# A Fourier mix and gated feed-forward kernel on one Trainium2 core: its first load units moved to partitions 16 to 111, and four edits beside it

## The chip, the cores and the metric

The kernel runs on one NeuronCore of a Trainium2 chip. The metric is the device time of one execution in microseconds (us), the median of several runs. The kernel before takes 2854.43 us (median of 3 runs, 2854.14 to 2856.18).

## What is computed

Two steps, all in float32. First a Fourier mix over the sequence of 3008 tokens, for 8 batches of 256 channels; then a feed-forward layer on the 24064 tokens that come out.

```python
X = np.fft.rfft(x, axis=1)                    # x: (8, 3008, 256)
Yr = Xr @ w_r - Xi @ w_i + b_r                # w_r, w_i: (256, 256)
Yi = Xr @ w_i + Xi @ w_r + b_i
Yr = np.sign(Yr) * np.maximum(np.abs(Yr) - 0.01, 0.0)
Yi = np.sign(Yi) * np.maximum(np.abs(Yi) - 0.01, 0.0)
y = np.fft.irfft(Yr + 1j * Yi, n=3008, axis=1)
gate = 1.0 / (1.0 + np.exp(-(y @ w_gate)))    # w_gate, w_val: (256, 1536)
val = y @ w_val
out = gate * val @ w_out                      # w_out: (1536, 256)
```

## The kernel before

The transform of length 3008 is split as 47 x 64. **Product a** (`fwd_a`, `product_a`, the line that the profile names `pa`) multiplies a unit of x by the 47-point table `fa_sb` on TensorE. A unit is a tile `xf` of 94 partitions (47 points x 2 halves) by 4 x 256 values, some 4 KB for each partition; a batch has 8 units. A unit takes two matmuls of 512 columns, each written to one PSUM bank (tag `fft`, three banks in turn) and copied back over the unit, the first by ScalarE, the second by VectorE, as 96 partitions. `store_a` then writes the unit to a DRAM buffer `zd`. **Step b** (`load_b`, `fwd_b`, tiles `zf` and `pb`) reads `zd` across all eight units, so its first load must wait until all eight units of its batch have been stored. It is followed by the mix with w_r and w_i (`mix4`, tile `pm`), the soft threshold and the inverse step (`inv_b`, tile `pi`), whose results go to `vd`. The last inverse product (`inv_a`, tile `pia`) reads `vd` as tiles `vf`, and makes the columns of y. Batch 0 goes through b, mix and inverse in 14 steps q, with batch 1's first product done beside it.

The feed-forward weights arrive as raw 64-bit words, in 18 parts of 512 KB (`load_part`, tiles `raw`), and VectorE and ScalarE make float32r high and low parts of them in some ten operations each (`from_f64`: the ops "exp", "top", "low" and so on). Seven parts go through the buffers of batch 0's units during the 14 steps, the eighth through the pool `big` (five buffers, which batch 1's units use as well). The others are loaded in the first chunk of the feed-forward, one for each of its 12 sub-steps f. `converting`, called three times in each `ffn1`, finishes the part in hand and starts the next; it stands ahead of the sigmoid in ScalarE's queue.

Since PE waits in the first chunk for weights, the first product of batches 2 and 3 is mixed in as filler: 32 **half units** (`load_half`, `half_a`; tiles `xfh` of 94 x 512 and `azh`, a ring of three buffers with tag `st`, stored by GpSimd's queue). `AT_FIRST` of them run ahead of the chunk's first `inv_a`; the others follow in the sub-steps.

The order of this part is written out by hand (`tc.manual_schedule()`): each engine runs its instructions in program order, and so does SP, which issues nearly all loads and stores. An instruction that waits holds everything behind it on its engine or queue. Fourteen matmuls on zeros (`warm`, `WARM`) stand ahead of the first product.

The lines in question:

```python
def load_a(b, h):                                             # L165
    xf = p0.tile([P, 4, D], F32, name="xf0", bufs=R1 // 8) if b == 0 else big("xf")
    for lo_, hi_ in ((0, 64), (64, 2 * R2)):
        nc.sync.dma_start(xf[lo_:hi_], xv[b, lo_:hi_, 4 * h:4 * h + 4])
...
    for h in range(na):                                       # L833
        load_a(0, h)
    load_a(1, 0)
    for h in range(na):
        fwd_a(0, h)
        store_a(0, h)
        if h in (1, 3, 4):
            load_a(1, {1: 1, 3: 2, 4: 3}[h])
```

Of the kernel before, what the change touches and what calls it, by code (L numbers as in the profile page):

```python
# [9 lines left out]
F32 = mybir.dt.float32  # L10
# [9 lines left out]
R2, R1 = 47, 64  # L20
NK2 = 24
NQ = 2 * NK2
# [9 lines left out]

SIDE_GAP = 14
PRE = 2
WARM = 14
EARLY = 4
AT_FIRST = 4
NCONV = 7


# [23 lines left out]
def _tables(seq):  # L64
    n2 = np.arange(R2)
    k2 = np.arange(NK2)
    c, s = _cs(n2[:, None] * k2[None, :], R2)
    fa = np.zeros((R2, 2, NK2, 2, 2))
    fb = np.zeros((NK2, 2, 2, 128))
    for j in range(2):  # L70
        fa[:, j, :, 0, j] = c
        fa[:, j, :, 1, j] = -s
        fb[:, 0, j, j:2 * R2:2] = c.T / seq
        fb[:, 1, j, j:2 * R2:2] = -s.T / seq
    fa = fa.reshape(2 * R2, 2 * NQ)
    fb = fb.reshape(2 * NQ, 128).astype(np.float32)
    n1 = np.arange(R1)
    k1 = np.arange(R1)
    mf = np.zeros((NK2, 128, 128), np.float32)
    mi = np.zeros((NK2, 128, 128), np.float32)  # L80
    mis = np.zeros((NK2, 128, 2, 128), np.float32)
    for q in range(NK2):
        k = q + R2 * k1
        c, s = _cs(n1[:, None] * k[None, :], seq)
        flip = np.where(k > seq // 2, -1.0, 1.0)
        m = np.zeros((2, R1, 2, R1))
        m[0, :, 0] = c
        m[1, :, 0] = s
        m[0, :, 1] = -s * flip
        m[1, :, 1] = c * flip  # L90
        w = np.full(R1, 2.0)
        if q == 0:
            w[k > seq // 2] = 0.0
            w[(k == 0) | (2 * k == seq)] = 1.0
        e = np.zeros((2, R1, 2, R1))
        e[0, :, 0] = (w * c).T
        e[1, :, 0] = (-w * flip * s).T
        if q:
            e[0, :, 1] = (w * s).T
            e[1, :, 1] = (w * flip * c).T  # L100
        mf[q] = m.reshape(128, 128)
        mi[q] = e.reshape(128, 128)
        mis[q, :, 0], mis[q, :, 1] = _split(e.reshape(128, 128))
    return {"mf": mf, "mi": mi, "mis": mis, "fa": fa.astype(np.float32), "fb": fb}


@with_exitstack
def tile_fft_mix_ffn(ctx: ExitStack, tc, x, w_r, w_i, b_r, b_i, w_one, w_out, mf, mi, mis, fa, fb, out):
    nc = tc.nc
    B, S, D = x.shape  # L110
    P = 128
    CT = D // P
    NF = w_one.shape[0]
# [14 lines left out]
    p0 = p0s.enter_context(tc.tile_pool(name="p0", bufs=1, side="right"))  # L128
# [8 lines left out]
    def bank(name, tag="fft", bufs=FFT_BANKS):  # L137
        return (psf if tag == "fft" else psl).tile([P, 512], F32, tag=tag, bufs=bufs, name=name)
# [5 lines left out]
        return p2.tile([P, 2, D], F32R, tag="r2k", bufs=NR2K, name=name)  # L144

    fa_sb = cw.tile([2 * R2, 2 * NQ], F32, name="fa_sb")
    nc.scalar.dma_start(fa_sb, fa)

    zd = [tc.dram_tile([NQ, R1, D], F32, name=f"zd{b}") for b in range(B)]
    vd = [tc.dram_tile([NQ, R1, D], F32, name=f"vd{b}") for b in range(B)]  # L150
# [1 line left out]
    md = tc.dram_tile([NK2, P, 2, P], F32, name="md")  # L152
    yd = tc.dram_tile([CT, P, B * S - T0], F32, name="yd").rearrange("t p n -> p t n")
    xv = x.rearrange("b (n2 j h) c -> b (n2 j) h c", j=2, h=R1 // 2)
    zv = [z.rearrange("q (j h) c -> (q j) h c", j=2) for z in zd]
    vv = [v.rearrange("q (j h) c -> (q j) h c", j=2) for v in vd]

    held = {}
# [3 lines left out]
    def big(name):  # L162
        return p2.tile([P, 4, D], F32, tag="big", bufs=NBIG, name=name)

    def load_a(b, h):  # L165
        xf = p0.tile([P, 4, D], F32, name="xf0", bufs=R1 // 8) if b == 0 else big("xf")
        for lo_, hi_ in ((0, 64), (64, 2 * R2)):
            nc.sync.dma_start(xf[lo_:hi_], xv[b, lo_:hi_, 4 * h:4 * h + 4])
        held["x", b, h] = xf

    def product_a(xi, az, copy):
        pa = bank("pa")[:2 * NQ]
        nc.tensor.matmul(pa, fa_sb, xi, start=True, stop=True)  # L173
        copy(az, pa.rearrange("p (h c) -> p h c", h=2))

    def fwd_a(b, h):

        xf = held["x", b, h]
        for i in range(2):
            at = slice(2 * i, 2 * i + 2)  # L180
            product_a(xf[:2 * R2, at], xf[:2 * NQ, at], nc.vector.tensor_copy if b < 2 and i else nc.scalar.copy)

    def store_a(b, h, queue=nc.sync):
        queue.dma_start(zv[b][:, 4 * h:4 * h + 4], held.pop(("x", b, h))[:2 * NQ])

    def load_half(b, h):
        xf = r2k("xfh").bitcast(F32)
# [105 lines left out]
    def inv_b(b, q, m, full):  # L293
        pi = bank("pi")
        y = held.pop(("ys", b, q))
        for i in range(2):
            o = pi[:, i * D:(i + 1) * D]
            if full:
                nc.tensor.matmul(o, m[:, i], y[:, i], start=True, stop=True)
            else:  # L300
                yh, yl = y
                nc.tensor.matmul(o, m[:, i, 0], yh[:, i], start=True, stop=False)
                nc.tensor.matmul(o, m[:, i, 0], yl[:, i], start=False, stop=False)
                nc.tensor.matmul(o, m[:, i, 1], yh[:, i], start=False, stop=True)
        vz = p2.tile([P, 2, D], F32, tag="st", bufs=NST, name="vz")
        nc.scalar.copy(vz, pi.rearrange("p (q d) -> p q d", q=2))
        (nc.gpsimd if full else nc.sync).dma_start(vd[b][4 * q:4 * q + 4].rearrange("(q a) n d -> (a n) q d", q=2), vz)
# [514 lines left out]
    def halves(upto):  # L822

        while waiting:
            i = len(beside) - len(waiting)
            if i >= upto:
                break
            half_a(*waiting.pop(0))
            if i + NR2K < len(beside):
                load_half(*beside[i + NR2K])  # L830

    with tc.manual_schedule():
        for h in range(na):  # L833
            load_a(0, h)
        load_a(1, 0)
        for h in range(na):
            fwd_a(0, h)
            store_a(0, h)
            if h in (1, 3, 4):
                load_a(1, {1: 1, 3: 2, 4: 3}[h])  # L840
            if h == 2:
                load_mix()
        mfs[0] = load_mf(0)
        for q in range(2):
            load_b(0, q)
        load_bias4()
        mfs[1] = load_mf(1)
        for h in range(EARLY):
            fwd_a(1, h)
            if h == 1:  # L850
                wi_sb = mix_weights()
        for q in range(NP + 2):
            if q + 2 < NP:
                load_b(0, q + 2)
            if 0 <= q - 1 < NP:
                mis_[q - 1] = load_mi(q - 1, True)
            if q < 2:
                for h in range(q * EARLY // 2, (q + 1) * EARLY // 2):
                    store_a(1, h)
                load_part()  # L860
            if q == 3:
                nc.sync.dma_start(fb_sb, fb)
                load_bias()
            if len(parts) > 3 * NF // 2 - NCONV and q > 2 and q % 2 or q == NP:
                load_part()
            if q % 2 == 0 and 4 <= q < 4 + 2 * (na - EARLY):
                load_a(1, EARLY + q // 2 - 2)
            if q < NP:
                fwd_b(0, q, mfs[q], True)
            if q + 2 < NP:  # L870
                mfs[q + 2] = load_mf(q + 2)

            if q % 2:
                ops("sum word", 0)
                start_part(p0)
                ops("exp low top", -1)
            elif q:
                ops("power mant", -1)
                if len(started) > 1:
                    ops("hi lo", 0)  # L880
                ops("one", -1)
            if q == 4:
                sub(bias_sb[:, 1], bias_sb[:, 1], bias_sb[:, 0])
            if 0 <= q - 1 < NP:
                mix4(0, q - 1)
            if q == NP + 1:

                fwd_a(1, EARLY)
                store_a(1, EARLY, nc.gpsimd)
            if 0 <= q - 2 < NP:  # L890
                inv_b(0, q - 2, mis_[q - 2], True)

        for bh in beside[:NR2K]:
            load_half(*bh)
        left = ["hi lo", "power mant one", "sum word", "hi lo"]
        for h in range(EARLY + 1, na):
            ops(left.pop(0), 0)
            fwd_a(1, h)
            store_a(1, h, nc.gpsimd)
        ops(left.pop(0), 0)  # L900
    p0s.close()
    p3 = p3s.enter_context(tc.tile_pool(name="p3", bufs=2, side="right", reuse_waits="tile"))
    with tc.manual_schedule():
        for u in own0:
            load_v(u)
        halves(AT_FIRST)
        for f in range(NF):
            ffn[f]()
            if f in (2, 3):
                tables[f - 2, 1] = load_mi(f - 2, False)  # L910
            halves(AT_FIRST + (f + 1) * (len(beside) - AT_FIRST) // NF)
            if parts:
                load_part()
    hook.clear()


# [127 lines left out]
```

## Time and profile before

| | |
|---|---|
| median of 3 runs | 2854.43 us (2854.14 to 2856.18) |
| the profiled execution, own time | 2852.08 us |
| its span, first to last instruction | 2850.3 us |
| PE (TensorE matmul) busy | 2812.0 us, 99% |
| VectorE (DVE) busy | 2085.8 us, 73% |
| ScalarE (ACT) busy | 1318.3 us, 46% |
| GpSimd (POOL) busy | 709.1 us, 25% |
| mean granted TensorE clock | 0.996 of full speed |

The profile is one execution; times within it count from the span's start, and the execution's own time is 1.8 us more than the span. Everything that the change touches happens in the first 205 us. Busy shares hide waits there, so the views to read are the ones by stretch, the waits of PE, and the chain of work that ended last, which goes back from the last instruction to what released each step.

### The profile page before, as it was taken

The numbers are of one execution on the slowest core, as the hardware profiler recorded it, in microseconds if no ns is written. First come the engines' busy times: TensorE is split into PE (matmuls) and PEld (weight loads), VectorE is DVE, ScalarE is ACT, GpSimd is POOL, SyncE is SP. The second block draws the span as 40 slices with busy tenths as digits, with TensorE's granted clock in tenths as the row PEclk, the third lists the DMA queues.
The fourth block names the chain that finished last, engine by engine and source line by source line (L and its number), as shares of the span: only waits on it lengthen the run. The fifth ranks groups of instructions, "written<-read, shape, count | busy, mean of one in ns | idle before, by whom it ended". The sixth has DMA issues, their size and how long they took to land.

```text
span 2850.3 us, 38265 instructions
## 1 busy us (share of the span) xinstructions
PE 2812.0 (99%) x13882; PEld 2308.8 (81%) x13882; DVE 2085.8 (73%) x3110; ACT 1318.3 (46%) x2293; POOL 709.1 (25%) x638
## 2 busy tenths in 40 slices
PE   8899999999999999999999999999999999999999
PEld 6668888888899977888888888888888888888887
DVE  5668777667778625777777777777777777777776
ACT  4565555454455433444444444444444444444443
POOL 0211000003900001323333333333333333333321
PEclk9999999999999999999999999999999999999999
DMA  9776544655654471000000000000000000000000
GB/s 274 224 220 190 171 144 136 178 168 179 215 155 145 144 231 54 16 15 30 30 30 15 16 30 30 16 15 30 30 30 15 16 30 30 16 15 30 30 16 15
DMA packets 174509, 240.49 MB, mean 84 GB/s; under 512 B 15792, under 2 KB 126096, under 8 KB 174320
## 3 DMA queue, kind: packets, MB, share of 16 engines
q1 hardware_dynamic: 164816, 214.41, 24.5%
q0 software_dynamic: 9408, 23.60, 2.6%
q8 instruction: 110, 1.80, 0.3%
q14 instruction: 79, 0.65, 0.1%
q10 hardware_dynamic: 96, 0.04, 0.0%
HBM read 133.65 MB, written 104.33 MB: 83 GB/s over the span
## 4 chain that ended last, share of the span: by engine, by line
PE 91%; DVE 4%; DMA 3%; ACT 1%; issue 1%; SPq 0%; POOL 0%; ACTq 0%; DVEq 0%; POOLq 0%
PE pd L635 11%; PE pc L635 11%; PE pa L635 11%; PE po L607 7%; PE po L606 7%; PE po L605 7%; PE pb L635 5%; PE pm L265 5%; PE pia L334 3%; PE pb L231 3%; PE pa L173 3%; PE po L411 1%; PE po L412 1%; PE po L413 1%; PE pv L388 1%; PE pv L386 1%
## 5 line engine op out<-in xcount | busy, mean ns | idle before, releaser
L607 PE MATMUL po<-hl,w 128*128 128x512 f32 x912 | 362.5, 398 | 0.0
L606 PE MATMUL po<-hh,w 128*128 128x512 f32 x912 | 361.6, 397 | 0.0
L605 PE MATMUL po<-hh,w 128*128 128x512 f32 x912 | 360.8, 396 | 0.0
L694 POOL TENSOR_TENSOR c<-c,c 128x512 f32<-128x512 f32 x114 | 147.2, 1291 | 807.7 <-DVE c L690 633.8
L635 PE MATMUL pc<-s,w1h 128*128 128x512 f32 x912 | 284.1, 393 | 2.8 <-DVE v L669 2.8
L635 PE MATMUL pa<-a,w1h 128*128 128x512 f32 x912 | 284.2, 393 | 0.5 <-ACT u L661 0.5
L690 DVE TENSOR_TENSOR c<-u,pc 128x512 f32<-128x512 f32 x228 | 156.6, 687 | 115.5 <-PE pc L635 106.9
L665 DVE TENSOR_TENSOR u<-u,pb 128x512 f32<-128x512 f32 x228 | 155.3, 681 | 88.9 <-PE pb L635 62.7
L585 ACT CAST hh<-v 128x512 fp32r<-128x512 f32 x114 | 70.7, 620 | 306.2 <-DVE v L675 306.2
L607 PEld LDWEIGHTS po<-hl,w 128*128 128x128 f32 x912 | 171.5, 188 | 41.9
L605 PEld LDWEIGHTS po<-hh,w 128*128 128x128 f32 x912 | 172.0, 189 | 41.0
L635 PEld LDWEIGHTS pa<-a,w1h 128*128 128x128 f32 x912 | 171.1, 188 | 41.0 <-ACT u L661 0.9
L635 PEld LDWEIGHTS pc<-s,w1h 128*128 128x128 f32 x912 | 170.8, 188 | 41.3 <-DVE v L669 4.1
L606 PEld LDWEIGHTS po<-hh,w 128*128 128x128 f32 x912 | 171.0, 188 | 40.7
L589 POOL TENSOR_TENSOR hl<-c,hh 128x512 fp32r<-128x512 f32 x114 | 152.3, 1336 | 186.1 <-ACT hh L585 186.1
L265 PE MATMUL pm<-w_sb,xsh 128*128 128x256 f32 x1008 | 189.2, 287 | 0.3 <-DVE ys L271 0.3
L635 PE MATMUL pc<-s,w1l 128*128 128x512 f32 x456 | 177.4, 389 | 0.0
L635 PE MATMUL pa<-a,w1l 128*128 128x512 f32 x456 | 177.0, 388 | 0.0
L696 DVE TENSOR_TENSOR u<-u,pd 128x512 f32<-128x512 f32 x228 | 156.8, 688 | 24.5 <-DVE c L690 0.9
L667 DVE TENSOR_TENSOR v<-u,pd 128x512 f32<-128x512 f32 x228 | 156.8, 688 | 24.4 <-DVE u L665 0.5
L669 DVE TENSOR_TENSOR v<-v,pc 128x512 f32<-128x512 f32 x228 | 156.7, 687 | 24.4 <-DVE v L667 0.9
L661 ACT COPY u<-pa 128x512 f32<-128x512 f32 x228 | 133.7, 586 | 79.5 <-PE pa L635 79.3
(164 smaller groups left out, 6762.1 us busy)
## 6 DMA issues: line engine op xcount, KB each, us to landing
zf<-zd SPq DMA_DIRECT2D x96, 256.0 KB, 3.6
vf<-vd SPq DMA_DIRECT2D x128, 192.0 KB, 3.2
out_dram<-ot SPq DMA_DIRECT2D x94, 256.0 KB, 2.1
vd<-vz SPq DMA_DIRECT2D x84, 256.0 KB, 2.8
ypair<-yd SPq DMA_DIRECT2D x19, 1024.0 KB, 4.9
yd<-yf SPq DMA_DIRECT2D x103, 188.0 KB, 3.0
zd<-xf SPq DMA_DIRECT2D x44, 384.0 KB, 3.7
xf<-in_x_dram SPq DMA_DIRECT2D x48, 256.0 KB, 4.4
```

The costliest lines, as they stand in the source:

```text
L265: nc.tensor.matmul(o, l, r, start=(i == 0), stop=(i == len(mms) - 1))
L589: sub_(hl, h, hh)
L605: nc.tensor.matmul(o, wh, hh, start=(f == 0), stop=False)
L606: nc.tensor.matmul(o, wl, hh, start=False, stop=False)
L607: nc.tensor.matmul(o, wh, hl, start=False, stop=(f == NF - 1))
L635: nc.tensor.matmul(o, l, r, start=not more and l is wh and r is xh, stop=l is wl, skip_group_check=more)
L665: add(u, u, b)
L667: add(v, u, d)
L669: add(v, v, c)
L690: add(c12, u, c)
L694: nc.gpsimd.tensor_mul(c12, g12, c12)
L696: add(u, u, d)
```

## The change

- The units of batch 0, and the first four of batch 1, are loaded by one DMA of 96 rows to partitions 16 to 111, in place of two of 64 and 30 rows to partitions 0 to 93. Partitions 0 to 15 are set to zero by a memset (VectorE for the odd units of batch 0, GpSimd for all others), and the product uses a table `fa0_sb` of 128 x 128, shifted by 16 and with zeros around. The product now has 110 rows and 112 columns of weights, and its copies have 112 partitions. Of the 96 rows the last two belong to the next batch, and their table rows are not used. The other units still use `fa_sb`, which is now loaded in step q = 3.
- In SP's queue the first unit of batch 1 no longer stands ahead of the first store; batch 1's units follow stores 0, 2, 4 and 6, and w_r and w_i follow store 3.
- `WARM` goes from 14 to 10.
- One more weight part, the ninth, is loaded ahead of the chunk: after the 14 steps and before the first half units' loads. In the chunk the load of a part moves ahead of the half units of its sub-step.
- `AT_FIRST` goes from 4 to 3, so that 29 and not 28 half units run within the chunk.

```diff
-WARM = 14
+WARM = 10
 EARLY = 4
-AT_FIRST = 4
+AT_FIRST = 3
+AT0 = 16
...
+    fa0 = np.zeros((128, 128))
+    fa0[AT0:AT0 + 2 * R2, AT0:AT0 + 2 * NQ] = fa
...
     def load_a(b, h):
-        xf = p0.tile([P, 4, D], F32, name="xf0", bufs=R1 // 8) if b == 0 else big("xf")
+        xf = big("xf")
...
+    TOP = AT0 + 2 * NQ
+
+    def load_a0(b, h, clear):
+        xf = p0.tile([P, 4, D], F32, name="xf0", bufs=R1 // 8) if b == 0 else big("xf")
+        clear(xf[:AT0], 0.0)
+        at = b * 2 * R2
+        nc.sync.dma_start(xf[AT0:TOP], xr[at:at + 2 * NQ, 4 * h:4 * h + 4])
+        held["x", b, h] = xf
+
+    def fwd_a0(b, h):
+        xf = held["x", b, h]
+        for i in range(2):
+            at = slice(2 * i, 2 * i + 2)
+            product_a(xf[:AT0 + 2 * R2, at], xf[:TOP, at], nc.vector.tensor_copy if i else nc.scalar.copy,
+                      fa0_sb[:AT0 + 2 * R2, :TOP])
+
+    def store_a0(b, h):
+        nc.sync.dma_start(zv[b][:, 4 * h:4 * h + 4], held.pop(("x", b, h))[AT0:TOP])
...
         for h in range(na):
-            load_a(0, h)
-        load_a(1, 0)
+            load_a0(0, h, (nc.vector if h % 2 else nc.gpsimd).memset)
         for h in range(na):
-            fwd_a(0, h)
-            store_a(0, h)
-            if h in (1, 3, 4):
-                load_a(1, {1: 1, 3: 2, 4: 3}[h])
-            if h == 2:
+            fwd_a0(0, h)
+            store_a0(0, h)
+            if h % 2 == 0:
+                load_a0(1, h // 2, nc.gpsimd.memset)
+            if h == 3:
                 load_mix()
...
             if q == 3:
+                nc.sync.dma_start(fa_sb, fa)
                 nc.sync.dma_start(fb_sb, fb)
...
                 inv_b(0, q - 2, mis_[q - 2], True)
+        load_part()
 
         for bh in beside[:NR2K]:
             load_half(*bh)
...
-            halves(AT_FIRST + (f + 1) * (len(beside) - AT_FIRST) // NF)
             if parts:
                 load_part()
+            halves(AT_FIRST + (f + 1) * (len(beside) - AT_FIRST) // NF)
```

SP's queue at the start, from the last unit of batch 0 on, in the kernel before (`xf_145` is that unit, `xf` are units of batch 1, `xf_124` to `xf_130` the first three of batch 0, `zd_77` batch 0's buffer in DRAM; behind "waits" stand the semaphores of the queues and engines waited for):

```order
L168 DMA xf_145<-in_x_dram 64x1024 [waits DMAHW7_49]
L168 DMA xf_145<-in_x_dram 30x1024 [waits DMAHW0_49]
L168 DMA xf<-in_x_dram 64x1024 [waits DMAHW1_49]
L168 DMA xf<-in_x_dram 30x1024 [waits DMAHW2_49]
L184 DMA zd_77<-xf_124 96x1024 [waits DMAHW3_49,DVE_49,Activation_49]
L184 DMA zd_77<-xf_127 96x1024 [waits DMAHW4_49,DVE_49,Activation_49]
L168 DMA xf<-in_x_dram 64x1024 [waits DMAHW5_49]
```

The same place in the kernel changed (`xf_142` is the last unit, `xf_121` to `xf_130` the first four, `zd_78` the buffer):

```order
L200 DMA xf_142<-in_x_dram 96x1024 [waits DMAHW0_49]
L211 DMA zd_78<-xf_121 96x1024 [waits DMAHW1_49,DVE_49,Activation_49]
L200 DMA xf<-in_x_dram 96x1024 [waits DMAHW2_49]
L211 DMA zd_78<-xf_124 96x1024 [waits DMAHW3_49,DVE_49,Activation_49]
L211 DMA zd_78<-xf_127 96x1024 [waits DMAHW4_49,DVE_49,Activation_49]
```

Eight issues stand ahead of the first store now, where eighteen stood, and no load of batch 1 is among them.

SP's queue between the 14 steps and the first chunk, before (`raw` is a weight part, `xfh` a half unit, `vf` a load of `vd` for `inv_a`):

```order
L784 DMA raw<-in_w_out_dram 128x1024
L189 DMA xfh<-in_x_dram 64x512 [waits DMAHW2_49]
L189 DMA xfh<-in_x_dram 30x512 [waits DMAHW3_49]
...
L189 DMA xfh<-in_x_dram 30x512 [waits DMAHW1_49]
L317 DMA vf<-vd_85 96x512 [waits DMASW5_49,DMASW4_49,DMASW6_49,DMASW3_49,DMASW7_49,DMASW2_49,DMAHW2_49,DMASW1_49,DMASW0_49]
```

The same place now:

```order
L811 DMA raw<-in_w_out_dram 128x1024 [waits Pool_49]
L811 DMA raw<-in_w_one_dram 128x1024 [waits DMASW3_49,DMAHW7_49,DVE_49,Activation_49]
L216 DMA xfh<-in_x_dram 64x512 [waits DMAHW0_49]
L216 DMA xfh<-in_x_dram 30x512 [waits DMAHW1_49]
...
L216 DMA xfh<-in_x_dram 30x512 [waits DMAHW7_49]
L344 DMA vf<-vd_86 96x512 [waits DMASW5_49,DMASW6_49,DMASW4_49,DMASW7_49,DMASW2_49,DMAHW0_49,DMASW1_49,DMASW0_49]
```

The ninth part stands between the eighth and the half units' eight loads. It takes the `big` buffer of batch 1's fifth unit, and so waits for that unit's store on GpSimd's queue (DMASW3); the half units and the `vf` loads are queued behind it.

ScalarE's queue ahead of the chunk, before (`azh` are the copies of half units, `yth` the first operand of the feed-forward):

```order
L174 COPY azh<-pa 96x512 [waits DMASW1_49,PE_49]
L174 COPY azh<-pa 96x512 [waits DMASW2_49,PE_49]
L174 COPY azh<-pa 96x512 [waits DMASW4_49,PE_49,Activation_49]
L174 COPY azh<-pa 96x512 [waits DMASW0_49,PE_49]
L326 CAST yth<-pia 128x2x188 [waits PE_49] x2
```

And now:

```order
L181 COPY azh<-pa 96x512 [waits DMASW1_49,PE_49]
L181 COPY azh<-pa 96x512 [waits DMASW2_49,PE_49]
L181 COPY azh<-pa 96x512 [waits DMASW4_49,PE_49,Activation_49]
L353 CAST yth<-pia 128x2x188 [waits PE_49] x2
```

The fourth copy, which waited for the store of the first one's buffer (DMASW0), is no longer ahead of `yth`.

## Rows read from the trace of the kernel before

**Rows 1.** The page's part 5, a GpSimd operation: busy us, mean ns | idle, releaser.

```profile
L694 POOL TENSOR_TENSOR c<-c,c 128x512 f32<-128x512 f32 x114 | 147.2, 1291 | 807.7 <-DVE c L690 633.8
```

**Rows 2.** Stretches: length; busy us of each engine; PEclk, DMA share, GB/s.

```profile
2.20:14.00 11.80, 11.80 (x32) 6.04 (x31) 2.54 (x4) 3.61 (x5) 0.00 (x0) 1.00 1.00 247
33.38:43.00 9.62, 8.44 (x40) 8.18 (x41) 1.81 (x3) 4.13 (x8) 0.00 (x0) 0.54 0.93 304
43.00:95.80 52.80, 51.40 (x393) 48.79 (x392) 45.68 (x80) 34.47 (x63) 7.63 (x11) 1.00 0.85 255
130.10:134.57 4.47, 4.46 (x13) 3.50 (x14) 3.72 (x8) 2.82 (x6) 1.40 (x3) 0.62 0.39 126
205.00:2850.00 2645.00, 2627.34 (x13035) 2177.20 (x13034) 1960.96 (x2896) 1202.01 (x2083) 678.53 (x582) 1.00 0.23 72
```

**Rows 3.** Waits of PE, 0 to 210 us: releaser, total, times, longest.

```profile
PE pv L386 <- ACT sg L392: 4.0, 2, 3.7
PE pb L231 <- DMA zf<-zd: 3.7, 1, 3.7
PE pia L334 <- ACT azh L174: 3.0, 3, 2.0
...
PE pg L388 <- DVE w1l L770: 0.9, 1, 0.9
```

**Rows 4.** Timeline of PE, 0 to 13 us: start, length, instruction.

```profile
1.46 5.00 PE L811 MATMUL warm<-zero 128*128 128x512 f32 x14 [1.46 <-DVE ebias L817]
6.29 7.19 PE L173 MATMUL pa<-xf,fa_sb 94*96 94x512 f32 x16
```

**Rows 5.** Timeline of SP's queue, the issues of three stretches.

```profile
0.74 11.35 SPq L168 DMA_DIRECT2D xf<-in_x_dram  x18
12.66 0.79 SPq L184 DMA_DIRECT2D zd<-xf  x2
...
22.33 2.06 SPq L184 DMA_DIRECT2D zd<-xf  x3
...
93.06 4.58 SPq L189 DMA_DIRECT2D xfh<-in_x_dram  x8
...
103.28 1.44 SPq L317 DMA_DIRECT2D vf<-vd  x3
```

**Rows 6.** The DMA view, 22.5 to 29.5 us.

```profile
DMA packets 832, 2.56 MB, mean 366 GB/s; under 512 B 136, under 2 KB 217, under 8 KB 832
```

**Rows 7.** The chain that ended last, 20 to 45 us: start, length, what.

```profile
24.09 6.27 DMA zd<-xf
...
30.50 2.75 DMA zf<-zd
```

**Rows 8.** The chain, 104 to 131 us.

```profile
111.81 2.03 PE pia L334 x8
...
115.58 0.43 PE pg L388
...
117.62 0.23 PE pv L387
...
122.61 5.60 DMA raw<-in_w_one_dram
```

**Rows 9.** GpSimd's store of batch 1's fifth unit: its issue, and its time to landing.

```profile
98.94 0.55 POOL L184 DMA_DIRECT2D zd<-xf  x1 [2.59 <-ACT xf L174]
...
DMA to landing us min/median/max: 3.2/3.2/3.2
```

**Rows 10.** Time to landing: half unit loads issued at 93.1 and 93.6, then last two vf.

```profile
DMA to landing us min/median/max: 3.9/4.1/4.3
...
DMA to landing us min/median/max: 4.9/4.9/5.0
```

**Rows 11.** Timeline of PE, 102 to 115 us.

```profile
103.66 3.60 PE L173 MATMUL pa<-xfh,fa_sb 94*96 94x512 f32 x8
...
114.31 0.79 PE L386 MATMUL pg<-yth,w1h 128*128 128x512 f32 x1 [0.47 <-ACT yth L326]
```

More of the change, by code (lines that the diff above doesn't have):

```diff
@@ L76, in _tables @@
     fb = fb.reshape(2 * NQ, 128).astype(np.float32)
+    fa0 = np.zeros((128, 128))
+    fa0[AT0:AT0 + 2 * R2, AT0:AT0 + 2 * NQ] = fa
+    fa0 = fa0.astype(np.float32)
     n1 = np.arange(R1)
@@ L103, in _tables, with tile_fft_mix_ffn @@
         mis[q, :, 0], mis[q, :, 1] = _split(e.reshape(128, 128))
-    return {"mf": mf, "mi": mi, "mis": mis, "fa": fa.astype(np.float32), "fb": fb}
+    return {"mf": mf, "mi": mi, "mis": mis, "fa0": fa0, "fa": fa.astype(np.float32), "fb": fb}
 @with_exitstack
-def tile_fft_mix_ffn(ctx: ExitStack, tc, x, w_r, w_i, b_r, b_i, w_one, w_out, mf, mi, mis, fa, fb, out):
+def tile_fft_mix_ffn(ctx: ExitStack, tc, x, w_r, w_i, b_r, b_i, w_one, w_out, mf, mi, mis, fa0, fa, fb, out):
     nc = tc.nc
@@ L146, in tile_fft_mix_ffn @@
     fa_sb = cw.tile([2 * R2, 2 * NQ], F32, name="fa_sb")
-    nc.scalar.dma_start(fa_sb, fa)
+    fa0_sb = p0.tile([P, P], F32, name="fa0_sb")
+    nc.scalar.dma_start(fa0_sb, fa0)
     zd = [tc.dram_tile([NQ, R1, D], F32, name=f"zd{b}") for b in range(B)]
@@ L154, in tile_fft_mix_ffn @@
     xv = x.rearrange("b (n2 j h) c -> b (n2 j) h c", j=2, h=R1 // 2)
+    xr = x.rearrange("b (n h) c -> (b n) h c", h=R1 // 2)
     zv = [z.rearrange("q (j h) c -> (q j) h c", j=2) for z in zd]
@@ L169, in load_a, with product_a @@
         held["x", b, h] = xf
-    def product_a(xi, az, copy):
-        pa = bank("pa")[:2 * NQ]
-        nc.tensor.matmul(pa, fa_sb, xi, start=True, stop=True)
+    def product_a(xi, az, copy, table=None):
+        pa = bank("pa")[:az.shape[0]]
+        nc.tensor.matmul(pa, fa_sb if table is None else table, xi, start=True, stop=True)
         copy(az, pa.rearrange("p (h c) -> p h c", h=2))
@@ L848, in tile_fft_mix_ffn @@
         for h in range(EARLY):
-            fwd_a(1, h)
+            fwd_a0(1, h)
             if h == 1:
@@ L858, in tile_fft_mix_ffn @@
                 for h in range(q * EARLY // 2, (q + 1) * EARLY // 2):
-                    store_a(1, h)
+                    store_a0(1, h)
                 load_part()
             if q == 3:
+                nc.sync.dma_start(fa_sb, fa)
                 nc.sync.dma_start(fb_sb, fb)
```

## The prediction

> **What bounds it now.** I read the busy time by stretch first. From 205 us to the end PE is busy for 2627 of 2645 us at full clock [rows 2]: what is won or lost ahead of that moves the end by as much, and little can be won behind it. So the question is PE's losses in the first 205 us, and the waits of PE name three [rows 3]: 3.7 us for `zf`, the first load of step b; 3.0 us for ScalarE's copies of half units (2.0 of it at one place, ahead of the first chunk); and 3.7 us of one wait for a sigmoid in the chunk. Next I read the clock. From 33.38 to 43.0 us PE's mean clock is 0.54, that is nearly all at 1.2 GHz in place of 2.4, after the wait for `zf`; from 130.10 to 134.57 it is 0.62, after the wait for the sigmoid [rows 2]. The 14 steps of batch 0 between them (43.0 to 95.8 us) keep PE busy for 51.4 of 52.8 us. Last, the chain says what each wait hangs on.
>
> At the start it is the last store of batch 0, issued at 24.09 and landed 6.27 us later; then `zf`, issued at 30.50 and landed in 2.75 [rows 7]. The store is late because DMA is full: from 2.2 to 14 us, nearly all x loads, its share is 1.00 at 247 GB/s [rows 2], while from 22.5 to 29.5 us, mostly stores of 96 partitions, 366 GB/s flow [rows 6]. Besides, SP issues loads until 12.1 us and the first store at 12.66 [rows 5]. In the chunk the chain goes through a raw part, issued at 122.61, landing after 5.60 us [rows 8]: ScalarE stood waiting for it with the sigmoid behind.
>
> **The start.** Ahead of the last store's landing stand 12 unit loads of 385 KB, 8 stores of 393 KB and 0.52 MB of w_r and w_i, 8.3 MB. The new loads have 96 rows, so it becomes 12 x 0.393 + 8 x 0.393 + 0.52 + 0.07 (the table) = 8.46 MB. What rate do loads of 96 rows get? No row shows them alone. Bounds: 247 GB/s, as the loads of 64 and 30 rows get now, and 400, a tenth above the 366 of the stores [rows 2, 6]; I take 366, since the new loads have the stores' shape (96 partitions, 4 KB each). From 2.2 us on, 8.46 MB / 366 take 23.1 us, so 25.3. The 8.3 MB of now, 13.8 us at 247 and the other 4.9 MB at 366, end at 29.4, and the last store lands at 24.09 + 6.27 = 30.4 [rows 7], 1.0 us behind its data; so the store lands at 26.3. `zf` takes 0.14 + 2.75 + 0.13 us as now [rows 7], and step b starts at 29.3 in place of 33.38: **-4.1 us**. At 400 GB/s VectorE's six weight operations ahead of the last unit copies decide, at about 27.7: -5.7. With loads at 247 and the rest at 366, 19.1 + 10.2 us of data: +2.1.
>
> PE is no bound of this. Its warm-up takes 1.46 to 6.46 us for 14 matmuls [rows 4]; at 0.23 us for each of the last four, as at full clock [rows 8], 10 end near 5.5. From 6.29 on the product runs at 7.19 / 8 = 0.90 us [rows 4], two to a unit, so the last unit of batch 0 is done near 20, and its store lands only at 26.3. The shorter warm-up would save its 0.9 us at most, and I count nothing: DMA is the cover, and if that went, 0.9 us would be gained. The products follow the warm-up without a gap in either kernel, so the clock should rise as it does now.
>
> The memsets: GpSimd's two-input operation on 512 columns takes 1.29 us [rows 1], so one of 1024 columns takes at most 2.6; four end by 11 us, and the unit of the last is needed near 16. VectorE's first copy is due at 6. Copies of 112 partitions in place of 96, and 110 rows in the product, have the same columns: nothing. `fa_sb` at q = 3 is one more issue on SP, in a stretch with DMA share 0.85 [rows 2]: nothing, and 0.5 us if it lands on a needed `zf`.
>
> With the wait shorter (PE's products end near 27, `zf` comes at 29.3) the clock may fall later or not at all. But the second and third product of step b hang on loads behind it in SP's queue, so I count **-0.5 us** of the slow stretch, between 0 and -2.
>
> **Ahead of the chunk.** Here SP is made to wait. The ninth part waits for the fifth unit's store, issued at 98.94 and landed 3.2 us later [rows 9], so at 102.1. Behind it are the half units' eight issues, 4.58 us [rows 5], which ran at 93.06 and now start at 102.5. The first half unit lands about 4.3 us later [rows 10], near 106.8; PE has run out of work at 103.66 [rows 11] and stands for 3 us. The `vf` loads, issued at 103.28 now [rows 5], come at 107.1; the last of three takes 1.0 us to its issue and 4.9 to land [rows 10], 113.0. The third `pia`, which waits for the fourth half unit's copy and runs at 111.81 now [rows 8], starts there: what the removed copy gives, the `vf` load takes back, and the chunk starts **+1.2 us** late. It stays slow for longer after such a pause: before, seven of the first twelve matmuls take 0.43 us and five 0.23 [rows 8]; with all at 0.43, **+1.0**. The half unit moved into the chunk, where PE has no gap, costs two matmuls of 0.43 us, **+0.9**.
>
> In return the ninth part is there when the second sub-step asks for it, and the 3.7 us go [rows 3]: **-3.7**. The stretch at 1.2 GHz behind it, 4.47 us for twelve matmuls, becomes 12 x 0.23 = 2.8 [rows 2, 8]: **-1.7**. What is late next is PE itself: a sub-step has 18 matmuls of 0.23 us and two or three half units, and the tenth part is issued behind the third `vf`, 10 us before it is asked for. Later parts come earlier too; of the 0.9 us that PE waited for one [rows 3], **-0.5**.
>
> The sum is -4.1 - 0.5 + 1.2 + 1.0 + 0.9 - 3.7 - 1.7 - 0.5 = **-7.4 us** on the profiled execution's 2852.08 us, 2844.7. The median of the runs is 2.35 us above that execution, so 2847.0. About 0.2%, 5.7 us, is what a measurement of this kernel can tell from no change; the forecast is just beyond it, at -0.26%.
>
> **Rivals.**
>
> *Loads stay slower than stores.* They write to the on-chip memory where stores read from it, and only stores have shown 366 GB/s. Midway, at 308, the twelve loads take 15.3 us and the rest 10.2; step b starts at 31.7, -1.7 in place of -4.1, and the sum is -5.0: 2849.4. For it: the 247 of the loads alone; against it: 366 was reached with the last units' loads among the stores. [...]
>
> *The ninth part's wait eats the gain at the chunk.* If the halves and `vf` loads land another 2 us later, and the clock stays at 1.2 GHz for one more sub-step, the place gives 0 or +1 in place of -2.3: sum -4.5, 2849.9. For it: ScalarE and PE have no other work there.
>
> *Slower.* The move to partitions 16 to 111 makes all these DMAs, stores too, as slow as the loads are now. At 247 GB/s 8.46 MB take 34.3 us; step b starts at 40.5, +7.1 us, and with a pause of 13 us the clock is low for two sub-steps more, +2. With the -3.3 of the rest the sum is +5.8: 2860.2. It decides at an average below 310 GB/s, where the start is no earlier than now. Against it: stores of 96 partitions run at 366, and nothing in the trace makes partition 0 a better start than 16.
>
> *It does not act.* The order of SP's and ScalarE's instructions shows each edit in place, so this has no chance of its own.
>
> **How the numbers follow.** Forecast 0.58; slower loads 0.19; the chunk's gain eaten 0.18; slower 0.05. The forecast's own spread (start -5.7 to -2, chunk -4.5 to 0) puts some of its chance within 0.2%, and some of the rivals' beyond. Faster by over 0.2% (below 2848.7): 0.60. Within: 0.36. Slower: 0.04. The range takes the start at -5.7 with the clock up (-2) and the chunk at -4.5 below (-12.7 with the -0.5 of later parts: 2841.7), and both first rivals at once above (-2.1: 2852.3), and 1.7 us at each end for the runs' own spread of 2.0 us: 2840 to 2854.
>
> **What would show it.** Right: the DMA view of the first 11 us well above 300 GB/s; the first store issued near 8 us; `pb` starting near 29; SP standing at the ninth part until 102 less the gain so far, PE idle for some 3 us ahead of the half units; and no wait of `pv` for a sigmoid above 1 us. Wrong: x loads still near 250 GB/s, `pb` after 32, or a new wait of PE in the 14 steps.

## The result and the profile after

The changed kernel takes 2861.83 us (median of 15 runs, 2856.49 to 2868.46); the kernel before, on the same chip beside it, 2855.28 us (15 runs, 2852.25 to 2862.7). The ratio is 1.0019, with a 95% interval of 1.0011 to 1.0028: 5.4 us slower, which is clear of no change by the interval and just under the 0.2% that the prediction counted as no change. The forecast was 0.26% faster, and its range ended at 2854. Single runs of one kernel spread over some 10 us here, so small differences below are read from ratios over many runs, and from the place in the trace where they arise.

| | before | after |
|---|---|---|
| profiled execution, own time | 2852.08 us | 2861.69 us |
| span | 2850.3 us | 2859.6 us |
| PE busy | 2812.0 us | 2816.8 us |
| mean granted clock | 0.996 | 0.993 |

First four stretches of the changed kernel, then the last two of them in the kernel before (length; busy us of PE, its loads, VectorE, ScalarE, GpSimd; clock, DMA share, GB/s):

```profile
2.20:14.00 11.80, 11.57 (x29) 5.53 (x28) 5.78 (x8) 3.80 (x6) 5.71 (x7) 1.00 1.02 233
43.00:95.80 52.80, 51.39 (x391) 48.90 (x392) 45.58 (x80) 35.23 (x65) 7.62 (x11) 1.00 0.89 262
95.80:123.80 28.00, 20.57 (x55) 11.75 (x54) 10.68 (x19) 10.66 (x20) 5.05 (x9) 0.70 0.65 210
180.00:200.00 20.00, 15.00 (x51) 9.71 (x50) 12.27 (x22) 12.29 (x23) 2.71 (x6) 0.83 0.48 150
```

```profile
95.80:123.80 28.00, 24.03 (x80) 14.24 (x79) 13.35 (x23) 14.57 (x27) 6.56 (x12) 0.88 0.69 217
180.00:200.00 20.00, 18.21 (x71) 11.58 (x69) 12.84 (x23) 13.55 (x26) 3.55 (x7) 1.00 0.84 239
```

The first row answers to the first of [rows 2]: the wide loads fill the DMA engines as the narrow ones did (share 1.02) and move 233 GB/s, not the 366 that I took. The second says that the 14 steps are as before. The third and fourth hold the new losses: PE stands for 7.4 us ahead of the chunk, where it stood for 4.0 in the kernel before, and for 5.0 us in the chunk's tenth sub-step, where it stood for 1.8, and the clock is lower in both. The waits of PE from 80 to 210 us name both, and show that the 3.7 us for the sigmoid [rows 3] are gone:

```profile
PE pa L180 <- DMA xfh<-in_x_dram: 6.1, 1, 6.1
PE pa L180 <- ACT carry L373: 5.0, 1, 5.0
...
PE pv L413 <- ACT sg L419: 0.2, 1, 0.2
```

**The start.** PE's timeline up to step b, which answers to [rows 4] and the `pb` of [rows 2]:

```profile
1.46 3.90 PE L838 MATMUL warm<-zero 128*128 128x512 f32 x10 [1.46 <-DVE zero L835]
5.60 15.92 PE L180 MATMUL pa<-xf,fa_sb 110*112 110x512 f32 x36 [0.23 <-DMA fa_sb<-in_fa_dram]
22.57 1.94 PE L180 MATMUL pa<-xf,fa_sb 110*112 110x512 f32 x4 [1.06 <-DMA xf<-in_x_dram]
26.96 2.47 PE L180 MATMUL pa<-xf,fa_sb 110*112 110x512 f32 x4 [2.44 <-DMA xf<-in_x_dram]
...
33.73 1.77 PE L258 MATMUL pb<-mf_sb,zf 128*128 128x128 f32 x8
```

PE's first product starts 0.7 us earlier, then PE waits for batch 1's units, and `pb` starts at 33.73, where it stood at 33.38. The chain says why: the last store is issued 0.8 us earlier than before, but takes 7.55 us to land in place of 6.27 [rows 7], so it is there at 30.84 in place of 30.36. PE itself is busy with batch 1's last unit until 33.68, at a matmul time of 0.93 us (the clock from 30 to 33.38 us is 0.50), so the low clock came mostly ahead of step b here: from 33.38 to 43 us it is 0.91, in place of 0.54 [rows 2].

```profile
23.29 7.55 DMA zd<-xf
```

**Ahead of the chunk.** SP's queue, then PE's timeline of the same place; they answer to [rows 5] and [rows 11]. Between them stand SP's wait at the ninth part and, from the chain, the way of the first half unit:

```profile
91.46 0.46 SPq L811 DMA_DIRECT2D raw<-in_w_out_dram  x1
102.36 0.34 SPq L811 DMA_DIRECT2D raw<-in_w_one_dram  x1
102.75 6.44 SPq L216 DMA_DIRECT2D xfh<-in_x_dram  x8
109.48 1.25 SPq L344 DMA_DIRECT2D vf<-vd  x3
```

```profile
SPq L811 <- DMA zd<-xf: 10.3, 1, 10.3
```

```profile
103.56 6.19 DMA xfh<-in_x_dram
```

```profile
98.08 5.75 PE L180 MATMUL pa<-xf,fa_sb 94*96 94x512 f32 x12 [0.79 <-DVE xf L181]
109.89 5.41 PE L180 MATMUL pa<-xfh,fa_sb 94*96 94x512 f32 x6 [6.06 <-DMA xfh<-in_x_dram]
115.09 5.27 PE L361 MATMUL pia<-fb_sb,vf 96*128 96x94 f32 x24
120.83 0.79 PE L413 MATMUL pg<-yth,w1h 128*128 128x512 f32 x1 [0.47 <-ACT yth L353]
```

SP stands at the ninth part for 10.3 us, until the fifth unit's store has landed. The first half unit comes 6.19 us after its issue at 103.56, while the 512 KB of the part are on their way too; without the part's read ahead of them, the half units' loads of the run below took 2.7 to 4.8 us, and the eight of the kernel before 3.0 to 4.3. PE idles 6.06 us, runs three half units in 5.41 us where four took 3.60 (the granted clock from 107 to 124 us is 0.51), and the chunk's first product starts at 120.83 in place of 114.31.

**In the chunk.** ScalarE, then VectorE, around the wait for the carry:

```profile
187.58 0.29 ACT L353 CAST yth<-pia 128x168 fp32r<-128x168 f32 x1
190.01 0.33 ACT L373 COPY carry<-pia 128x208 f32<-128x208 f32 x1 [2.13 <-DVE ytl L354]
```

```profile
187.71 0.69 DVE L427 TENSOR_TENSOR hl<-sg,hh 128x512 fp32r<-128x512 f32 x1 [0.68 <-ACT hh L426]
188.32 0.69 DVE L794 TENSOR_TENSOR raw<-raw 128x512 f32<-128x512 f32 x1
189.04 0.69 DVE L795 TENSOR_TENSOR raw<-raw,cv_e 128x512 f32<-128x512 f32 x1
189.65 0.33 DVE L354 TENSOR_TENSOR ytl<-pia,yth 128x168 fp32r<-128x168 f32 x1
```

With `AT_FIRST` at 3 the half units of the twelve sub-steps are 2, 2, 3, 2, 3, 2, 2, 3, 2, 3, 2, 3; at 4 they were 2, 2, 3 four times over. The tenth sub-step (f = 9), whose inverse product spans two chunks and leaves a `carry`, now has three. The three share the banks of tag `fft` with that product, which holds its bank until ScalarE has copied the carry; ScalarE waits for `ytl`, and `ytl` stands in VectorE's queue behind the conversion of a weight part. The third half unit waits 5.0 us for the bank, where before the next one waited 0.5.

Behind 205 us the two programs do the same. As a milestone for what follows I use the start of the last group of half units in the chunk (three half units in every kernel): 197.72 us before and 203.82 after, 6.1 us later. The spans of the two profiled executions differ by 9.3 us, so 3.2 us lie behind the milestone. The clock is at 0.89 on average from 785 to 800 and from 1065 to 1080 us, around waits of PE of 1.7 and 2.1 us for the inverse products' input, which makes some 1.7 us each time (0.11 x 15). Waits of that length stand in other profiled executions too, one of 2.6 us in the run with the order alone, so I take them for the spread between executions; that is not shown.

### The profile page after: what moved, and what is told of

The parts are those of the page before. It is cut to its first block, busy times and chain, and to the rows that moved or that the text cites. A ratio compares the mean times of both kernels' runs of the same rounds, so it can differ in the third digit from the quotient of the medians.

```text
span 2859.6 us, 38267 instructions
## 1 busy us (share of the span) xinstructions
PE 2816.8 (99%) x13878; PEld 2313.1 (81%) x13878; DVE 2090.0 (73%) x3114; ACT 1318.3 (46%) x2293; POOL 717.3 (25%) x646
## 4 chain that ended last, share of the span: by engine, by line
PE 91%; DMA 3%; DVE 3%; ACT 1%; issue 1%; SPq 0%; POOL 0%; DVEq 0%; ACTq 0%; POOLq 0%
PE pd L662 11%; PE pc L662 11%; PE pa L662 11%; PE po L634 7%; PE po L633 7%; PE po L632 7%; PE pb L662 5%; PE pm L292 5%; PE pia L361 3%; PE pb L258 3%; PE pa L180 2%; PE po L438 2%; PE po L439 2%; PE po L440 2%; PE pg L413 2%; PE pv L415 1%
```

## The experiments

The changes were taken apart: the front part (loads, memsets, table, warm-up), the order in the chunk (part ahead of half units), the ninth part's read, and the three half units.

**The front part alone** (edits on the changed kernel, which leave only the front part):

```diff
-AT_FIRST = 3
+AT_FIRST = 4
...
-        load_part()
...
+            halves(AT_FIRST + (f + 1) * (len(beside) - AT_FIRST) // NF)
             if parts:
                 load_part()
-            halves(AT_FIRST + (f + 1) * (len(beside) - AT_FIRST) // NF)
```

> The kernel before with the front part of the change alone: first units on partitions 16 to 111 with one DMA each, warm-up of 10 products; the parts are read and the half units dealt out as before. Theory A (the loss is made at the ninth part's read and by the half units' new distribution; the front is worth nothing, since the wide loads ran at 233 GB/s and the two traces coincide at 82.7 us): within 2 us of the kernel before. Rival B (the front itself loses, by its later products and the clock at the start): 4 to 7 us slower than before, which would be most of the loss of the whole change. Rival C (the front gains the 4 us forecast, and the rest loses 10): 4 us faster than before.

Measured: 0.9998 of the kernel before (0.9988 to 1.0009), milestone 196.92. Theory A holds: the front is worth nothing that the runs can measure, to some 3 us. The traces do show an earlier start:

```profile
31.30 1.13 PE L258 MATMUL pb<-mf_sb,zf 128*128 128x128 f32 x8 [1.71 <-DVE xf L181]
```

Step b starts at 31.30 here, and at 31.23, 31.45 and 32.81 in the three runs below with the same front part, against 33.38, 33.76 and 34.04 in the three kernels with the old one. The changed kernel's 33.73 is the latest of its five; the means are 32.1 and 33.7, so in these eight profiled executions the front part brings step b some 1.6 us earlier on average. What became of that by the end is not shown. The wait for the sigmoid is there, in two pieces:

```profile
PE pv L413 <- ACT sg L419: 5.3, 2, 3.5
```

**Without the ninth part's read:**

```diff
                 inv_b(0, q - 2, mis_[q - 2], True)
-        load_part()
```

> The changed kernel without the ninth weight part's read ahead of the half units; the parts are still read ahead of the half units inside the chunk, and three half units are still filler. Theory A: SyncE no longer stands 10.3 us at that read, the 3 us at the half units' input and most of the 6.5 us that the first chunk began late come back, with the clock lost behind it: 6 to 9 us faster than the changed kernel, 2 to 5 us faster than the kernel before if the gain at the products that waited for the sigmoid stays. Rival: the read ahead is what takes that wait away, so without it the wait returns, and the time falls by less than 4 us. In both, the 5.0 us wait of the third half unit for the carry's copy in the first chunk stays.

Measured: 0.9983 of before (0.9973 to 0.9993), so 0.36% or 10.3 us faster than the changed kernel; milestone 194.21. That is a little more than theory A's 6 to 9. The wait for the sigmoid did not come back, though the ninth part was no longer read early. The wait for the carry stayed:

```profile
PE pa L180 <- ACT carry L373: 4.0, 1, 4.0
```

**Four half units as filler, all else changed:**

```diff
-AT_FIRST = 3
+AT_FIRST = 4
```

> The changed kernel with four half units as filler again in place of three, so that the half units of the sub-steps stand as before (2, 2, 3, 2, 2, 3 and so on). Theory A: the 5.0 us wait of a half unit's product for the carry's copy at 185 us and the 6.8 us at 1.2 GHz behind it (worth half) go: 5 to 8 us faster than the changed kernel. Rival (the wait is only where earlier lateness is taken up, and stands elsewhere when it is taken away there): within 2 us of the changed kernel.

Measured: 1.0003 of before (0.9991 to 1.0014), 0.16% or 4.6 us faster than the changed kernel, a little under theory A's 5 to 8. The wait for the carry is gone. The profiled execution, 2861.96 us, was the slowest of the 11, and its milestone of 203.46 says little: it has a second wait for half units in the chunk besides the one for the first (12.1 us in two).

**Three half units in the kernel before:** `AT_FIRST` from 4 to 3 and nothing else.

> The kernel before with three half units as filler in place of four, nothing else. Theory A (the new distribution puts a third half unit into the sub-step whose inverse unit leaves a carry, and that waits): a wait of about 5 us of a half unit's product for the carry's copy and lower clock behind it, 4 to 8 us slower than before, less the 0.9 us of the half unit moved. Rival (the wait comes from the parts' reads being moved): no such wait, within 2 us of the kernel before.

Measured: 1.0009 of before (0.9999 to 1.0019), milestone 201.62, 3.9 us later. Theory A's wait is there without any part's read moved. Its cost is 2.6 us by the runs, below the 4 to 8 expected, and their interval includes no change; so the wait is shown by the trace, and its price hardly by the runs.

```profile
PE pa L173 <- ACT carry L346: 5.6, 1, 5.6
```

**Front part and order, without the other two:** the edits of the two kernels above it that drop the ninth read and set `AT_FIRST` to 4.

> The changed kernel without the ninth part's read and with four half units as filler: what is left of the change is the front part and, inside the chunk, each part's read ahead of the half units. Theory A: neither the 10.3 us stop of SyncE nor the wait for the carry's copy is there, and the gate's products no longer wait for the sigmoid (5.3 us in the run with the front part alone): 2 to 6 us faster than the run with three half units and no ninth read (that one stood at 0.9983 of before), so 0.996 to 0.998 of the kernel before. Rival (the products wait for the sigmoid because of the half units' place, and three as filler cured it): the wait is back and the time is that of the kernel before within 2 us.

Measured: 0.9967 of before (0.9956 to 0.9979), milestone 191.07. Theory A holds, and PE has no wait for the sigmoid.

**The order alone, in the kernel before:**

```diff
-            halves(AT_FIRST + (f + 1) * (len(beside) - AT_FIRST) // NF)
             if parts:
                 load_part()
+            halves(AT_FIRST + (f + 1) * (len(beside) - AT_FIRST) // NF)
```

> The kernel before with nothing but each part's read put ahead of the half units inside the chunk. Theory A (the order of these two alone cures the wait of the gate's products for the sigmoid, 4.0 us, and the low clock behind it): 3 to 6 us faster than before. Rival 1 (it was the ninth part, read earlier, that cured it): within 2 us of before, the wait still there. Rival 2 (the half units' reads, now behind a part, come late): slower.

Measured: 0.9972 of before (0.9960 to 0.9984), 8.0 us faster, milestone 189.34 (in the slowest of its 12 executions). Theory A holds, with more than its 3 to 6 us, and PE has no wait for the sigmoid. SP's queue shows it: the first part of the chunk is issued 8 us earlier than in the kernel before (122.61 in [rows 8]), since it no longer stands behind half units' loads that wait for their buffers.

```profile
114.60 0.36 SPq L784 DMA_DIRECT2D raw<-in_w_one_dram  x1
119.90 2.52 SPq L189 DMA_DIRECT2D xfh<-in_x_dram  x4
122.59 0.35 SPq L784 DMA_DIRECT2D raw<-in_w_one_dram  x1
```

**What sets the rate of a load.** The kernels that follow were read in the stretch 4 to 12 us, where nearly all traffic is loads of x; those that were only read for this ran once each. First the first units on partitions 0 to 95:

```diff
-AT0 = 16
+AT0 = 0
...
-        clear(xf[:AT0], 0.0)
```

> The changed kernel with its first units on partitions 0 to 95 in place of 16 to 111; the eight memsets ahead of the loads fall away. Read in the stretch 2.2 to 14 us of the span. Theory A (the loads of x go at a rate of their own, whatever the partitions): 230 to 265 GB/s, as in the kernels so far. Rival (the choice of partitions sets the rate of a load): another rate by more than 15%, at 0 to 95 either as fast as the stores (366 GB/s) or slower than 220.

```profile
4.00:12.00 8.00, 7.97 (x19) 3.28 (x19) 1.64 (x3) 3.03 (x4) 0.00 (x0) 1.00 1.05 251
```

The changed kernel itself has 233 in this stretch, and the four kernels with its front part 239 to 264: no effect of where the 96 rows lie is seen. Then 128 rows:

```diff
-        clear(xf[:AT0], 0.0)
...
-        nc.sync.dma_start(xf[AT0:TOP], xr[at:at + 2 * NQ, 4 * h:4 * h + 4])
+        nc.sync.dma_start(xf, xr[at:at + P, 4 * h:4 * h + 4])
```

> The changed kernel with the loads of its first units widened to 128 rows on all 128 partitions (12 loads of 512 KB in place of 384 KB; partition 16 and those above get rows of x that lie 16 further on, so its first units compute other rows). Read in the stretch 2.2 to 14 us. Theory A (the 16 transfer engines are full and each moves a load's bytes at a fixed rate): the same 230 to 265 GB/s, so each load takes a third longer and the last product of the first batch comes about 4 us later. Rival (a load's time is set by each partition's 8 KB, the partitions side by side): the same time for one load and 310 GB/s or more.

```profile
4.00:12.00 8.00, 8.00 (x19) 3.57 (x19) 1.95 (x3) 3.04 (x4) 0.00 (x0) 1.00 1.02 411
```

411 GB/s (375 from 2.2 to 14 us): theory A falls, and the rival's "310 or more" is exceeded. With a third more bytes a load takes less time than one of 96 rows (512 KB at 411 in 1.28 us, 384 KB at 233 to 264 in 1.69 to 1.49). So this was built on the kernel before, with the better order: one DMA of 128 rows for each of the first units, the rows too many left unused.

```diff
-WARM = 14
+WARM = 10
...
-        for lo_, hi_ in ((0, 64), (64, 2 * R2)):
-            nc.sync.dma_start(xf[lo_:hi_], xv[b, lo_:hi_, 4 * h:4 * h + 4])
+        for lo_, hi_ in ((0, 128),) if b < 2 else ((0, 64), (64, 2 * R2)):
+            nc.sync.dma_start(xf[lo_:hi_], xr[b * 2 * R2 + lo_:b * 2 * R2 + hi_, 4 * h:4 * h + 4])
```

> The kernel before with each part's read ahead of the half units, a warm-up of 10 products, and the loads of the first units (batches 0 and 1) as one DMA of 128 rows on partitions 0 to 127 in place of 64 and 30 rows; the 34 rows too many are read and not used. Theory A (a 128-row load runs at over 400 GB/s, as in the run that widened them, so the transfers no longer hold the start): 380 GB/s or more in the stretch 4 to 12 us, the first product of step b 1 to 3 us earlier than the 34.0 us of the run with the order alone, and the time 0 to 3 us under that run: 0.996 to 0.9975 of the kernel before. Rival (the start is bound by the products and the way of the last unit through DRAM, not by the loads): the rate rises and step b starts at 33 us or later, time as with the order alone within 1 us.

Measured: 0.9964 of before (0.9952 to 0.9977), median 2843.71 us. Its rate, and its step b:

```profile
4.00:12.00 8.00, 7.82 (x19) 3.32 (x19) 1.84 (x3) 3.03 (x4) 0.00 (x0) 1.00 1.02 405
```

```profile
32.16 1.68 PE L232 MATMUL pb<-mf_sb,zf 128*128 128x128 f32 x8 [3.67 <-DMA zf<-zd]
```

Step b starts 1.9 us before the 34.04 of the order alone, and the milestone, 186.30, is 3.0 us earlier. So theory A's rate and start came; its gain in time is not shown, since the runs cannot tell the two apart: 0.9964 and 0.9972, with intervals that overlap. It has the lowest ratio of the kernels tried, and is ahead of both kernels of the change beyond its interval; what is shown of that is the order's gain, while the loads' share rests on the trace.

**The half units' loads with 128 rows as well:** in `load_half` one DMA `xr[b * 2 * R2:b * 2 * R2 + P, 2 * h:2 * h + 2]`.

> The run before with the half units' loads as one DMA of 128 rows too, in place of 64 and 30. SyncE issues 32 DMAs fewer, and 4 of the 8 that stand ahead of the inverse units' loads at the first chunk (4.58 us for 8 before). Theory A (the first chunk's start hangs on these issues): the inverse units' input and the first product of the gate come up to 2 us earlier, 0 to 3 us faster than the run without it. Rival (its start hangs on the unit a products and the way of the inverse units' rows through DRAM): no change within 1 us, or slower, since 36% more bytes are read for the half units.

Measured: 0.9968 of before (0.9957 to 0.9980): no difference from the kernel without it that the runs can tell. The first product of the gate starts at 112.98 us, where it started at 111.53 without, so not earlier; both are as the rival said, though the runs alone do not exclude a gain of a microsecond or two.

**Two DMAs of 64 rows:** in the kernel with 128 rows, `((0, 64), (64, 128))` in place of `((0, 128),)`.

> As the run with 128-row loads, but each in two DMAs of 64 rows (partitions 0 to 63 and 64 to 127). Read in the stretch 4 to 12 us. Theory A (what makes a load fast is that all 128 partitions are written by the loads in flight): 380 GB/s or more, though each DMA has half the rows. Rival (it is the number of rows of one DMA): 230 to 270 GB/s, as with 64 and 30 rows.

```profile
4.00:12.00 8.00, 6.97 (x16) 2.80 (x16) 1.37 (x2) 2.63 (x4) 0.00 (x0) 1.00 1.03 229
```

229 GB/s, the rival: what counts is the single DMA, not that all partitions are written by the loads in flight. These DMAs are also smaller, 256 KB in place of 512, but the size alone does not explain it. The loads of `zf` are single DMAs of 256 KB to all 128 partitions, and while two of them land, with two loads of 64 KB beside them, the kernel before moves 335 GB/s:

```profile
32.00:33.50 1.50, 0.12 (x1) 0.15 (x1) 0.00 (x0) 0.00 (x0) 0.00 (x0) 0.51 0.97 335
```

**112 rows:** `((0, 112),)`.

> As the run with 128-row loads, but with 112 rows (partitions 0 to 111). Read in the stretch 4 to 12 us. Theory A (the rate grows with the share of the partitions that a load fills): between the 229 to 258 GB/s of 96 rows and the 400 to 422 of 128, about 300 to 350. Rival (only a load on all 128 partitions is fast): 230 to 270.

```profile
4.00:12.00 8.00, 7.75 (x18) 3.20 (x18) 1.37 (x2) 3.03 (x4) 0.00 (x0) 1.00 1.04 278
```

278, between the two expectations and nearer to the rival's: 448 KB in 1.65 us, as long as 96 rows take, so nearly all of the step comes with the last 16 rows.

## Why the prediction was wrong

The parts add up. Taken from the ratios, in us of 2855: the front part -0.6; the order, added to it, -8.8; three half units, added to these, +4.6; the ninth read, added last, +10.3; together the +5.4 of the change, by construction. What tests it is the other way round: with four half units the ninth read costs 0.36% too (1.0003 against 0.9967), and the three half units 0.16% beside the ninth read too. Each of these steps is uncertain by some 4 us, from intervals of about 3 us to either side of each ratio: the order and the ninth read are clear of that, the three half units barely. Of the steps of the prediction that failed, the price of the ninth read is the largest (2.2 us forecast, 10.3 measured), then the rate of the loads, then the half unit's price.

- **The start, -4.1 and -0.5: wrong.** The step that failed is "I take 366, since the new loads have the stores' shape". Loads of 96 rows got 233 to 264 GB/s, about what those of 64 and 30 rows get (237 to 247). I had 247 as the lower bound; the shape was the wrong analogue, the direction and the row count the right ones. My rival of loads at 308 kept the same error in part. But the +2.1 that my sum gives at 247 did not come either: step b starts 0.35 us later in the changed kernel, and 1.6 us earlier in the mean of the five with its front part. The sum has no term for the new order in SP's queue. With it the first store is issued at 8.41 to 9.58 us (8 was forecast) in place of 12.66 to 13.35, and from 14 to 22.5 us, where loads and stores are mixed, the five kernels move 337 to 405 GB/s, the three with the old front part 321 to 333. That the order is the reason is read from the traces and was not tried alone. The shift by 16 partitions bought nothing that the runs show: 251 GB/s at 0 to 95, 233 to 264 at 16 to 111.
- **The warm-up, nothing: right.** PE started 0.7 us earlier and waited for units later.
- **The ninth part's wait, +1.2 and +1.0: the mechanism right, the size off by nearly a factor of five.** SP did stand, until 102.24 (I had 102.1). Then two terms were too small. "The first half unit lands about 4.3 us later" came from [rows 10], where the 512 KB of the eighth part had been issued 1.6 us earlier (91.45); with those of the ninth issued 0.4 us earlier (102.36) it landed after 6.19, and the pause was 6.1 and not 3 us. And I let the half units run at full clock after the pause: at 0.90 us a matmul in place of 0.45, and with the inverse products slow too, they pushed the chunk's start to 120.83, where I had 115.5. The runs give 10.3 us for this read. The rival of the eaten gain had the place and the direction, but took 2.3 to 3.3 us more than the forecast, where 8 were needed.
- **The half unit moved, +0.9: mis-sized, for a reason that I did not see.** I priced two matmuls. The edit also redistributes the others, and puts a third one where a bank is held: a wait of 5.0 us, by the runs 4.6 us beside the order and 2.6 alone, neither far from their spread.
- **The wait for the sigmoid, -3.7, -1.7 and -0.5: the size about right, the cause wrong.** I wrote "the ninth part is there when the second sub-step asks for it". The order inside the chunk does it alone, with 8.0 us against the 5.9 forecast. The ninth read, to which I gave the gain, only costs once the order is there; without the order it was not tried.
- **What would show it.** Of the signs that I had named as wrong, loads near 250 GB/s and `pb` after 32 both came; of those named as right, the first store near 8 us, SP at the ninth part until 102 and no wait of `pv` above 1 us.
- **The chances.** By its ratio the result lies within 0.2%, to which I gave 0.36, but on the slow side and outside the range. My one way to a slower kernel was a slow DMA everywhere. The way that happened lay in two places that I had costed at small numbers and not asked how far they could go: an in-order queue behind a store, and a table of numbers that moves other work than the one meant.

## What to carry to other kernels

When a load is moved ahead in an in-order queue, price the buffer that it takes: everything behind it waits for that buffer's last reader, and here it cost 10.3 us where the reordering alone gave 8.0. When a count sets a distribution, write the whole distribution out and look at each place where it puts more. Read a transfer's rate from transfers of the same direction and row count; where data is loaded in fewer than 128 rows and DMA is full, try one DMA of 128 rows with the surplus unused; here the transfers of the first units went by it from 246 GB/s, with 64 and 30 rows, to 405, and a gain in the kernel's time was not shown.

## What the runs showed of the hardware

- With 4 KB a row, loads of 64, 96, 112 and 128 rows in one DMA ran at 229, 233 to 264, 278 and 405 to 411 GB/s, each with the DMA engines' share at 1.02 to 1.05; a stretch of mostly stores of 96 rows ran at 366 [rows 6]. Why 96 rows can be stored at such a rate and not loaded was not tried.
- The pause of PE ahead of the chunk cost about as much again behind it. From 95.8 us to the first `pv` the kernel before took 21.49 us, 17.52 of it busy, at a mean clock of 0.84; the changed kernel took 28.00, 20.57 of it busy, at 0.70. Of the 6.5 us more, 3.5 are idle and 3.0 slower products, though it ran one half unit fewer.
- The profile gives the granted clock as a share of full speed, so the frequencies in the prediction are estimates. In the kernel before, at a share of 0.50 (34 to 42 us), three matmuls of 256 columns take 0.64 us (39.10 to 39.74), 1.2 columns a ns, which by the share makes 2.4 at full speed; at 1.00 three of them take 0.35 us (44.26 to 44.61), 2.2 columns a ns.
- More partitions cost the first products and their copies next to nothing, as the prediction has it: in the median a copy of 112 partitions took 0.585 us on ScalarE and 0.692 on VectorE, one of 96 partitions 0.581 and 0.687, and a matmul with 110 rows 0.593 us, with 94 rows 0.592. The memsets took 0.94 us on GpSimd and 0.91 on VectorE.
